# Which tiles share a round of A at the start: tiles 1 and 2 of layer 1 together, and layer 1 three tiles ahead of layer 3 from the first pair on

## The chip, the core and the metric

The kernel runs on one core of one Trainium2 chip, as one launch. The metric is device time in microseconds of a whole execution; the median of three runs before the change is 2122.01 us (2117.99 to 2125.99). TensorE is called PE below, VectorE DVE, ScalarE ACT, GpSimd POOL, and SyncE SP, which issues most DMAs.

## The reference, cut to what matters

The input is a sequence of 2048 rows of 576 values. Four layers are applied one after the other, each with a layer norm before it and a residual sum after it:

```
x = x + A(layernorm(x))     # layer 1
x = x + B(layernorm(x))     # layer 2
x = x + A(layernorm(x))     # layer 3
x = x + B(layernorm(x))     # layer 4
```

A is a local attention with 32 heads of 18: `qkv = x @ wqkv`, then each row attends to itself and to the seven rows that lie 2, 4, ... 14 rows before it, then `@ wo`. B walks the sequence in 64 segments of 32 rows. It has 32 heads of 128. For each segment it puts 8 memory rows ahead of the 32 rows, computes q, k, v, scores with softmax, and the output projection with `Wo`; the first 8 output rows are the memory of the next segment, so segment s+1 cannot begin before segment s has ended. Both A layers use the same weights, and so do both B layers.

## The kernel before

**Steps of B.** The main loop runs over 69 steps. In step t, layer 2 handles segment t (lane 0) and layer 4 handles segment t-5 (lane 1; `DLY=5`), side by side in the same matmuls. A step has the q and k projection of 11 groups of heads (`qk`, lines 908 and 911), the v projection (`vpass`, line 955), scores and softmax for two halves of the heads (`scores`, lines 995 to 1005, and `softmax`, lines 844 to 865), probabilities times v (`pv`, line 1046), and the output projection (`oproj`, line 1070). All weights of B stay in SBUF.

**Rounds of A.** A works on tiles of 64 rows, two steps of B each. One call of `a_tile` is a round, with one or two tiles (`parts`, pairs of layer and tile number). With two tiles, each matmul of the projection (line 570) has 128 columns in place of 64, so both tiles share the weight loads. The weights of A do not stay in SBUF: `wload` brings them as ten strips through `ring`, which has two buffers; strips 0 to 6 are wqkv and 7 to 9 are wo. The first use takes them from a place inside `wo`, where they are put at the start; the second and third use gather them again from the inputs, and the third also stores a packed copy; from the fourth on one DMA fetches the packed copy. In a round the attention (`a_attend`) runs tile after tile: products of q and k in `big` (one buffer), sums over heads on PE (line 678), softmax, a spread of the weights back over the channels on PE (line 703), products with v, and sums. `a_out` then applies wo (line 747), adds the residual, stores x, and makes the normed input of B (`xnb`) through a second layer norm (line 469). A tile needs the last 14 rows of k and v of the tile before it, in `halo1` or `halo3`.

**Which round has which tiles.** `trace` (line 1138) makes the list `its`. Three rounds hold one tile each: 0, 1 and 2 of layer 1. Then tile j+3 of layer 1 is paired with tile j of layer 3 for j = 0, 1, 2. A round with tile 6 alone follows (`EXTRA`), and from there tile j+4 is paired with tile j of layer 3. In the rounds marked late (the second entry of an item), the wo part of the layer 1 tile is held over (`self.pend`) and done together with the layer 3 tile of the next round; so from tile 6 on one `a_out` has two tiles as well. There are 36 rounds and 38 wo parts.

**What sets the order.** Nothing is issued in the order of the source. Every piece is registered with `pl.op`: engine, planned duration, priority, what it depends on, and what buffers it takes. `_Plan.run` (line 93) then plays the whole program through once with these durations, lets each engine take the ready piece of the lowest priority number, and emits instructions in that order. So the order on each engine is fixed when the program is built. The priorities come from the table `PR` (line 1180): some 40 entries, with separate values for the first 12 steps (`_e`) and the last 8 (`_l`), picked by `_at`. PE has three array layouts in this kernel: full (F), four column groups (C: v projection, scores, line 678) and four row groups (R: `pv`, line 703); `mode` in `pl.op` names them, and the planner prefers to stay in one.

Of the kernel before, what the change touches and what calls it, by code (L numbers as in the profile page):

```python
# [27 lines left out]
T = 64  # L28
NS = T // SEG
# [213 lines left out]
AD_ = ("ACT", "DVE")  # L243


def _at(t):
    x = "_e" if t < EARLY else "_l" if t >= NSTEP - LATE else ""
    return {k: PR.get(k + x, v) for k, v in PR.items() if k[-2:] not in ("_e", "_l")}


class _K:
    def __init__(self, ctx, tc, A_x, A_wqkv, A_wo, B_mem0, B_Wq, B_Wk, B_Wv, B_Wo, out):
        self.ctx, self.tc, self.nc = ctx, tc, tc.nc
        self.A_x, self.A_wqkv, self.A_wo = A_x, A_wqkv, A_wo
        self.B_mem0, self.B_Wq, self.B_Wk, self.B_Wv, self.B_Wo = B_mem0, B_Wq, B_Wk, B_Wv, B_Wo
        self.out = out
        _, self.S, d = A_x.shape
        assert d == D and self.S % P == 0
        assert B_Wq.shape[1] == NH and B_Wq.shape[2] == P and B_mem0.shape[1] == NM
        self.NT = self.S // T  # L260
        self.NSEG = self.S // SEG
        self.dly = DLY
        self.nsteps = self.NSEG + self.dly
        assert self.nsteps == NSTEP
        self.scale_b = float(P) ** -0.5
        self.pl = _Plan()
        self.halo = {}


    def pool(self, name, bufs, space=bass.MemoryType.SB):  # L270
        return self.ctx.enter_context(self.tc.tile_pool(name=name, bufs=bufs, space=space))
# [251 lines left out]
    def a_tile(self, parts, late_, dep):  # L523
# [1 line left out]
        nc, pl = self.nc, self.pl  # L525
        m = len(parts)
        n = m * T
        jt = parts[0][1] if m == 1 and parts[0][0] == 1 else 9
        early = jt < 2
        p = _at(NS * parts[-1][1] + (NS if parts[-1][0] == 3 else -LEAD))  # L530
        due, span = (NS * jt - p["a1"], p["a1s"]) if jt < 3 else (NS * parts[-1][1] + (8 if parts[-1][0] == 3 else 0) - p["a"], p["asp"])

        def pr(f):
            return due - span * (1.0 - f)
# [23 lines left out]
        for b in range(14):  # L558
# [15 lines left out]
                      uses=[xn, *w] + ([] if fresh else [ps]), lat=None if c == 3 or b == 13 else 0.0, mm=5)  # L574
            if fresh and 0 < part < 3:
                for l, (layer, j) in enumerate(parts):
                    hin = self.halo.get(layer)

                    def hcopy(e, part=part, l=l, j=j, hin=hin):
                        h = dst[part].t[:, :, l, 0:HALO]  # L580
                        if j == 0:
                            nc.vector.memset(h, 0.0)
                        else:
                            self.copy(e, h, hin[0].t[:, part - 1])
                    got[part, "h", l] = pl.op("DVE" if j == 0 else ("POOL", "ACT") if early else "POOL", 0.25, hcopy, pr(Q[1]),
                                              [o] if j == 0 else [o, hin[1]], uses=[dst[part]] if j == 0 else [dst[part], hin[0]])
# [17 lines left out]
                    got[part, "r"] = pl.op(AD_, _evac(n), evr, pr(Q[1] + 0.08), [o], uses=[ps, dst[part]])  # L604
        pend, self.pend, out = self.pend, None, []
        dep = None
        for l, (layer, j) in reversed(list(enumerate(parts))):
            if j + 1 < self.NT:
                hk = pl.buf(f"halo{layer}")

                def hsave(e, hk=hk, l=l):
                    self.copy(e, hk.t[:, 0], kT.t[:, :, l, T:T + HALO])
                    self.copy(e, hk.t[:, 1], vT.t[:, :, l, T:T + HALO])
                oh = pl.op(("POOL", "ACT") if early else "POOL", 0.5, hsave, pr(Q[2]), [got[1], got[2], got[1, "r"], got[2, "r"]], acq=[hk], uses=[kT, vT])
                self.halo[layer] = (hk, oh)
            late = layer == 1 and late_
            if layer == 3 and pend is not None:
                oT, o_go = pend[4:6]
            else:
                oT = pl.buf("oT")  # L620
                o_go = pl.op("NONE", 0.0, None, pr(Q[0]), [gates[0], dep], acq=[oT])
            o_o, o_l = self.a_attend(layer, j, l, layer // 2, dst, oT, got, o_go, dep, pr, p[f"A{layer}"], early)
            dep = o_o
            it = (layer, j, xTs[l], o_o, oT, o_go, o_l)
            if late:
                self.pend = it
            else:
                out.append(it)
# [239 lines left out]
    def load_x(self, t):  # L868
# [1 line left out]
        nc, pl = self.nc, self.pl  # L870
        hT = pl.buf("hT")
        self.hT[t] = hT
        gate = pl.op("NONE", 0.0, None, t + _at(t)["lx"], [self.qk_op.get(t - 1)], acq=[hT])
        self.x_in[t] = {l: gate for l in range(2)}
        self.gate[t] = gate
        for l in range(2):
            s = self.lane_seg(t, l)
            if s is None:
# [1 line left out]
            xnb, dep = self.xn_ready[l][s // NS]  # L880
            self.x_in[t][l] = pl.op(("POOL", "ACT"), (0.35, 0.36),
                                    lambda e, l=l, s=s, xnb=xnb: self.copy(e, hT.t[:, :, XC[l]:XC[l] + SEG], xnb.t[:, s % NS]),
                                    t + _at(t)["lx"], [dep, gate], uses=[hT, xnb])
            if l == 0 and t % 2 == 0:
                self.x_ahead = pl.op(("POOL", "ACT"), (0.26, 0.29),
                                     lambda e, s=s, xnb=xnb: self.copy(e, hT.t[:, :, W80:HW_], xnb.t[:, s % NS + 1, :, 0:HW_ - W80]),
                                     t + _at(t)["lx"], [dep, gate], uses=[hT, xnb])
            if s == 0:
                m0 = MC + l * NM
                o = pl.op("ACT", 0.26, lambda e, m0=m0: self.copy(e, hT.t[:, :, m0:m0 + NM], self.mem0T[:]),  # L890
# [220 lines left out]

    def b_step(self, t):
        self.qkt, self.qk_ev, self.PT, self.ot, self.o_ev = {}, {}, {}, {}, []
        pr = {k: v[t % 2] for k, v in _at(t).items() if isinstance(v, tuple) and len(v) == 2}
        if t == 0:
            self.vpass(t, 2, 0.0)
        for g in range(11):
# [20 lines left out]
    def trace(self):  # L1138
# [4 lines left out]
        self.hT, self.x_in, self.mem_in, self.qk_op, self.V, self.v_ev, self.e_, self.gate = {}, {}, {}, {}, {}, {}, {}, {}  # L1143
        self.prologue()
        self.pend = None
        its, n1 = [([(1, j)], False) for j in range(3)], 3
        for j in range(NT):
            if j == EXTRA:
                its.append(([(1, n1)], True))
                n1 += 1  # L1150
            its.append((([(1, n1)] if n1 < NT else []) + [(3, j)], j >= EXTRA and n1 < NT))
            n1 += 1
        nl = 0
        for t in range(self.nsteps):
            while nl < len(its) and t >= (NS * its[nl][0][-1][1] + NS if its[nl][0][-1][0] == 3 else NS * its[nl][0][0][1] - LEAD):
                self.a_tile(*its[nl], self.qk_op.get(t - 1))
                nl += 1
            s = self.lane_seg(t - 1, 1) if t >= 1 else None
            if s is not None and s % NS == NS - 1:
                self.finish_out(s // NS, t + _at(t)["fin"])  # L1160
            for lane in range(2):
                s = self.lane_seg(t, lane)
                if s is not None and s % NS == 0:
                    self.residual(lane, s // NS, self.qk_op.get(t - 1), t + _at(t)["res"])
            if t == 0:
                self.load_x(0)
            self.b_step(t)
        self.finish_out(NT - 1, self.nsteps + _at(self.nsteps)["fin"])
        end, busy = pl.run(LOG)
        if VERBOSE:  # L1170
            print("planned", end, busy)
# [5 lines left out]
OTB = 1  # L1177
QKB = 6
RING = 2
PR = dict(qk=(0.307, -2.303), qkd=(0.12, 0.28), v1=(2.247, 4.528), v0=(-0.308, 18.626), s0=(1.899, 2.891), s1=(-11.667, -3.407),  # L1180
          p0=(-0.616, 1.782), p1=(-13.907, 1.038), o=(8.755, -1.999), od=(-3.184, -15.117), mo=(-19.565, -12.77), xo=(-3.022, -4.107),
          v2=(7.079, 5.525), wF=0.772, wC=-8.688, wR=-13.588, fin=2.628, res=-19.303, ring1=5.502, ring3=6.074, lx=16.523, rr=4.185,
          A1=(-16.669, 7.665, 23.282, 5.794, -6.099, 1.521, 0.493, 2.715), A3=(-15.249, 14.933, -15.849, -0.54, -6.577, -8.48, -12.203,
          1.866), a=3.872, asp=0.383, a1=5.649, a1s=-2.211, ai=13.867, st=4.522, qk_e=(2.072, -2.164), qk_l=(0.078, -3.139), qkd_e=(0.044,
          0.417), qkd_l=(0.162, 0.782), v1_e=(2.993, 3.224), v1_l=(2.805, 4.428), v0_e=(3.193, 17.29), v0_l=(-0.844, 18.276), s0_e=(2.324,
          1.847), s0_l=(2.213, -4.283), s1_e=(-10.888, -6.675), s1_l=(-18.328, -7.242), p0_e=(-5.597, 3.192), p0_l=(-8.936, 4.924),
          p1_e=(-21.304, 0.433), p1_l=(-16.629, -0.599), o_e=(15.149, -4.157), o_l=(8.314, -3.071), od_e=(-3.171, -15.728), od_l=(-3.404,
          -11.041), mo_e=(-18.961, -11.562), mo_l=(-14.457, -5.275), xo_e=(-7.103, -0.127), xo_l=(-5.204, -4.583), v2_e=(5.071, 6.422),
          v2_l=(7.565, 7.768), fin_e=1.864, fin_l=4.742, res_e=-16.965, res_l=-18.727, ring1_e=4.197, ring1_l=3.069, ring3_e=1.646,
          ring3_l=2.117, lx_e=10.885, lx_l=10.081, rr_e=6.184, rr_l=8.012, A1_e=(-10.347, 8.693, 24.271, 2.965, -6.696, 3.593, 1.284,  # L1190
          4.89), A1_l=(-6.983, 9.148, 25.195, 2.508, -11.699, 1.391, -0.388, -0.656), A3_e=(-14.483, 9.409, -19.943, -0.138, -3.201,
          -6.45, -15.079, -1.992), A3_l=(-11.391, 14.366, -19.827, 1.172, 1.674, -9.652, -8.623, -1.438), a_e=3.686, a_l=4.704,
          asp_e=0.219, asp_l=0.428, a1_e=3.433, a1_l=0.801, a1s_e=-0.01, a1s_l=-3.617, ai_e=11.156, ai_l=5.274, st_e=5.12, st_l=4.36)
LEAD = 5
EARLY = 12
LATE = 8
NSTEP = 69
EXTRA = 3
COPY = 2
HOLD = False  # L1200
# [58 lines left out]
```

## Time and profile before

| | |
|---|---|
| median of 3 runs | 2122.01 us |
| span of the profiled execution | 2120.6 us |
| PE busy | 2001.4 us (94%), 57787 matmuls |
| DVE, ACT, POOL busy | 1425.8 us (67%), 1169.1 us (55%), 808.5 us (38%) |
| DMA | 168.14 MB, mean 79 GB/s |
| fetches of strips of A, in packed form | 301 of 320 KB and 35 of 160 KB |

The page cuts the span into 40 slices of 53 us. The row of an engine gives its busy share in tenths. PE is a special case: matmuls are pipelined and each has a modelled end, so PE can be shown busy through a short wait. The start of a matmul to the start of the next is the surer measure. Steps are cut here at the first `qk` matmul of a step: the first is at 71.5 us, the sixth (step 6) at 245.3 us, step 12 at 454.7 us.

### The profile page before, as it was taken

How to read it: one execution, taken by the hardware profiler on the slowest of the kernel's cores; microseconds unless marked ns; L12 is line 12 of the kernel's file. 1: busy time of each engine (PE TensorE's matmuls, PEld its weight loads, DVE VectorE, ACT ScalarE, POOL GpSimd, SP SyncE). 2: the span in 40 equal slices, each digit the busy share in tenths (PEclk: the TensorE clock that was granted, in tenths of full speed). 3: DMA queues.
4: the chain of work that ended last, by engine and by line, in shares of the span. 5: the costliest groups of instructions: out<-in, count | busy, mean ns of one | idle time of the engine just before them, and what ended most of it. 6: DMA issues, size and time to landing. Idle time of an engine off the chain costs nothing. (4 is left out here: it accounts for less than half of the span.)

```text
span 2120.6 us, 126521 instructions
## 1 busy us (share of the span) xinstructions
PE 2001.4 (94%) x57787; PEld 1717.2 (81%) x57787; DVE 1425.8 (67%) x3839; ACT 1169.1 (55%) x2869; POOL 808.5 (38%) x1219
## 2 busy tenths in 40 slices
PE   1689989899999999999999999999999999999988
PEld 0468877788888888888888888888888888888876
DVE  2567756666677777776767667776767776766574
ACT  0345545565555555555556556555555555555553
POOL 2124434544434434434344434444344434322321
PEclk9999999999999999999999999999999999999999
DMA  9542223221222222221222212221222222212220
GB/s 322 158 125 77 66 93 96 81 75 54 68 78 78 76 67 68 70 62 59 69 78 77 75 61 74 66 62 60 75 78 76 69 66 70 67 55 73 65 74 13
DMA packets 100392, 168.14 MB, mean 79 GB/s; under 512 B 16904, under 2 KB 55824, under 8 KB 99728
## 3 DMA queue, kind: packets, MB, share of 16 engines
q1 hardware_dynamic: 94320, 140.88, 21.9%
q0 software_dynamic: 4576, 18.88, 2.6%
q8 instruction: 451, 7.39, 1.4%
q14 instruction: 85, 0.70, 0.1%
q10 hardware_dynamic: 960, 0.30, 0.1%
HBM read 144.06 MB, written 15.96 MB: 75 GB/s over the span
## 5 line engine op out<-in xcount | busy, mean ns | idle before, releaser
L908 PE MATMUL r<-hT,wq 128*128 128x80 bf16 (+1 forms) x8832 | 660.7, 198 | 7.6 <-ACT hT L280 6.6
L908 PE MATMUL r<-hT,wk 128*128 128x80 bf16 (+1 forms) x8832 | 663.3, 199 | 0.0
L908 PEld LDWEIGHTS <-wq 128*128 128x128 bf16 x8832 | 509.7, 99 | 22.3 <-issue 15.4
L280 ACT ACTIVATE qk<-r 128x480 bf16<-128x480 f32 (+2 forms) x688 | 364.6, 530 | 295.4 <-PE r L911 284.2
L911 PE MATMUL r<-hT,wqk_r 128*128 128x160 bf16 (+1 forms) x2208 | 508.0, 230 | 0.0
L908 PEld LDWEIGHTS <-wk 128*128 128x128 bf16 x8832 | 448.2, 100 | 0.0
L1070 PEld LDWEIGHTS <-wo 128*128 128x128 bf16 x11040 | 394.3, 100 | 41.6 <-issue 37.0
L1070 PE MATMUL r<-OT,wo 128*128 128x80 bf16 (+1 forms) x11040 | 411.7, 200 | 9.1 <-ACT OT L280 4.7
L287 POOL TENSOR_TENSOR big<-qT,kT 128x512 bf16<-128x512 bf16 x187 | 313.8, 1686 | 126.2 <-DVE oT L287 87.1
L955 PE MATMUL r<-wv,hT 128*32 128x512 bf16 x5376 | 355.0, 383 | 4.6 <-POOL hT L282 4.1
L287 POOL TENSOR_TENSOR ex<-ex,sum 128x320 bf16<-128x320 bf16 x136 | 105.8, 778 | 568.0 <-DVE sum L855 363.6
L955 PEld LDWEIGHTS <-hT 128*32 128x32 bf16 x6720 | 162.5, 96 | 140.2 <-POOL hT L282 4.3
L844 DVE TENSOR_REDUCE nmx<-r 128x8 f32<-128x320 f32 x276 | 133.7, 484 | 169.4 <-PE r L999 168.4
L280 ACT ACTIVATE V<-r 128x512 bf16<-128x512 f32 x281 | 167.6, 598 | 108.3 <-PE r L955 107.9
L911 PEld LDWEIGHTS <-wqk_r 128*128 128x128 bf16 x2208 | 220.1, 100 | 0.0
L280 ACT ACTIVATE OT<-r 128x320 bf16<-128x320 f32 (+1 forms) x401 | 145.6, 425 | 108.0 <-PE r L1046 107.6
L280 ACT ACTIVATE big<-r 128x384 bf16<-128x384 f32 (+1 forms) x316 | 117.9, 438 | 135.1 <-PE r L703 130.8
L287 POOL TENSOR_TENSOR xn<-x,st 128x256 bf16<-128x256 f32 x124 | 75.5, 629 | 271.4 <-DVE st L475 158.7
L570 PE MATMUL r<-xn,ring 128*128 128x128 bf16 (+1 forms) x2450 | 164.7, 215 | 10.6 <-DMA ring<-in_A_wqkv_dram 7.6
L570 PEld LDWEIGHTS <-ring 128*128 128x128 bf16 x2450 | 133.2, 98 | 19.5 <-DMA ring<-in_A_wqkv_dram 8.4
L845 DVE TENSOR_TENSOR r<-r,nmx 128x320 f32<-128x320 f32 x276 | 137.9, 500 | 9.5
L955 PE MATMUL r<-wv_r,hT 128*32 128x512 bf16 x1344 | 133.0, 381 | 0.0
(149 smaller groups left out, 2834.5 us busy)
## 6 DMA issues: line engine op xcount, KB each, us to landing
ring<-strip SPq DMA_DIRECT2D x301, 320.0 KB, 3.1
ring<-strip SPq DMA_DIRECT2D x35, 160.0 KB, 2.2
x1T<-x SPq DMA_DIRECT2D x32, 160.0 KB, 3.2
x<-x1T SPq DMA_DIRECT2D x32, 160.0 KB, 2.5
x3T<-x SPq DMA_DIRECT2D x32, 160.0 KB, 3.2
x<-x3T SPq DMA_DIRECT2D x32, 160.0 KB, 3.0
wo<-in_B_Wo_dram POOLq DMA_DIRECT2D x4, 1152.0 KB, 10.9
wq<-in_B_Wq_dram POOLq DMA_DIRECT2D x2, 2048.0 KB, 19.8
```

The source lines that it names most:

```text
L280: nc.scalar.activation(out=out, in_=in_, func=ACT.Copy, scale=1.0 if scale is None else scale)
L287: (self.nc.vector if e == "DVE" else self.nc.gpsimd).tensor_tensor(out=out, in0=in0, in1=in1, op=op)
L570: nc.tensor.matmul(ps.t[:, c * n:(c + 1) * n], lhsT=view()[:, kc, w0:w0 + P], rhs=xn.t[:, kc, 0:n], start=(kc == 0), stop=(kc == 4))
L844: nc.vector.tensor_reduce(out=m, in_=v, axis=AX.X, op=ALU.max, negate=True)
L845: nc.vector.tensor_tensor(out=v, in0=v, in1=m.unsqueeze(len(shp) - 1).to_broadcast(shp), op=ALU.add)
L908: nc.tensor.matmul(pv[:, hh, wi, a:b], lhsT=self.Wb[wi][0][:, kc, h * P:(h + 1) * P], rhs=hT.t[:, kc, a:b], start=(hh == 0 and wi == 0 and ...
L911: nc.tensor.matmul(pv[:, hh, :, a:b], lhsT=self.Wb[0][1][:, h * P:(h + 1) * P], rhs=hT.t[:, 4:6, a:b], start=False, stop=(hh == n - 1), sk ...
L955: nc.tensor.matmul(ps.t[c * 32:(c + 1) * 32, :], lhsT=l, rhs=w, start=(kc == 0), stop=(kc == 4))
L1070: nc.tensor.matmul(psY.t[:, mb * W80 + c0:mb * W80 + c1], lhsT=self.wo[:, w0:w0 + P], rhs=self.OT[:, h % 16 // 4 * 8 + h // 16 * 4 + h % 4 ...
```

## The change

The list of rounds becomes: tile 0 of layer 1 alone; tiles 1 and 2 of layer 1 in one round (`twin`); tile 3 alone, with its wo part held over; and then tile j+4 of layer 1 with tile j of layer 3 for all j, held over as long as there are layer 1 tiles. There are 35 rounds and 35 wo parts. All layer 1 rounds are registered at step 0, and their priorities come from `a1` and `a1s`. In the twin round the halo of the second tile is copied inside the round, from the last 14 rows of the first, and the two tiles are attended to in rising order. `_at` becomes the method `at` with the same rule. Nearly every number of `PR` is another one; what is computed, the sizes of all buffers, `DLY` and the planner are as before.

```
@@ a_tile
-        jt = parts[0][1] if m == 1 and parts[0][0] == 1 else 9
+        jt = parts[0][1] if parts[-1][0] == 1 else 9
+        twin = m == 2 and parts[1][0] == 1
-        p = _at(NS * parts[-1][1] + (NS if parts[-1][0] == 3 else -LEAD))
-        due, span = (NS * jt - p["a1"], p["a1s"]) if jt < 3 else (...)
+        p = self.at(NS * parts[-1][1] + NS if parts[-1][0] == 3 else 0)
+        due, span = (NS * jt - p["a1"], p["a1s"]) if jt < 9 else (...)
...
             if fresh and 0 < part < 3:
                 for l, (layer, j) in enumerate(parts):
+                    if twin and l == 1:
+                        continue
...
-        for l, (layer, j) in reversed(list(enumerate(parts))):
+        if twin:
+            for part in (1, 2):
+                got[part, "h", 1] = pl.op(("POOL", "ACT"), 0.25, lambda e, part=part: self.copy(
+                    e, dst[part].t[:, :, 1, 0:HALO], dst[part].t[:, :, 0, T:T + HALO]), pr(Q[1]), [got[part], got[part, "r"]], uses=[dst[part]])
+        for l, (layer, j) in list(enumerate(parts))[::1 if twin else -1]:
@@ trace
-        its, n1 = [([(1, j)], False) for j in range(3)], 3
-        for j in range(NT):
-            if j == EXTRA:
-                its.append(([(1, n1)], True))
-                n1 += 1
-            its.append((([(1, n1)] if n1 < NT else []) + [(3, j)], j >= EXTRA and n1 < NT))
-            n1 += 1
+        its = [([(1, 0)], False), ([(1, 1), (1, 2)], False), ([(1, 3)], True)]
+        its += [(([(1, j + 4)] if j + 4 < NT else []) + [(3, j)], j + 4 < NT) for j in range(NT)]
...
-            while nl < len(its) and t >= (NS * its[nl][0][-1][1] + NS if its[nl][0][-1][0] == 3 else NS * its[nl][0][0][1] - LEAD):
+            while nl < len(its) and t >= (NS * its[nl][0][-1][1] + NS if its[nl][0][-1][0] == 3 else 0):
@@ PR: nearly all entries, two lines of them
-          v2=(7.079, 5.525), wF=0.772, wC=-8.688, wR=-13.588, fin=2.628, res=-19.303, ring1=5.502, ring3=6.074, lx=16.523, rr=4.185,
...
+          2.879), p1=(-9.458, 0.493), o=(9.054, -2.393), od=(-2.489, -17.439), mo=(-22.332, -6.705), xo=(2.489, -5.463), v2=(9.677, 6.68),
+          wF=1.098, wC=-6.492, wR=-19.856, fin=2.968, res=-20.105, ring1=7.1, ring3=5.418, lx=7.005, rr=7.518, A1=(-18.916, 7.279, 17.403,
...
```

More of the change, by code (lines that the diff above doesn't have):

```diff
@@ L243 @@
 AD_ = ("ACT", "DVE")
-def _at(t):
-    x = "_e" if t < EARLY else "_l" if t >= NSTEP - LATE else ""
-    return {k: PR.get(k + x, v) for k, v in PR.items() if k[-2:] not in ("_e", "_l")}
 class _K:
@@ L263, in __init__ @@
         self.nsteps = self.NSEG + self.dly
-        assert self.nsteps == NSTEP
         self.scale_b = float(P) ** -0.5
@@ L267, in __init__, with at @@
         self.halo = {}
+    def at(self, t):
+        x = "_e" if t < EARLY else "_l" if t >= self.nsteps - LATE else ""
+        return {k: PR.get(k + x, v) for k, v in PR.items() if k[-2:] not in ("_e", "_l")}
     def pool(self, name, bufs, space=bass.MemoryType.SB):
@@ L527, in a_tile @@
         n = m * T
-        jt = parts[0][1] if m == 1 and parts[0][0] == 1 else 9
+        jt = parts[0][1] if parts[-1][0] == 1 else 9
+        twin = m == 2 and parts[1][0] == 1
         early = jt < 2
-        p = _at(NS * parts[-1][1] + (NS if parts[-1][0] == 3 else -LEAD))
-        due, span = (NS * jt - p["a1"], p["a1s"]) if jt < 3 else (NS * parts[-1][1] + (8 if parts[-1][0] == 3 else 0) - p["a"], p["asp"])
+        p = self.at(NS * parts[-1][1] + NS if parts[-1][0] == 3 else 0)
+        due, span = (NS * jt - p["a1"], p["a1s"]) if jt < 9 else (NS * parts[-1][1] + 8 - p["a"], p["asp"])
         def pr(f):
@@ L872, in load_x @@
         self.hT[t] = hT
-        gate = pl.op("NONE", 0.0, None, t + _at(t)["lx"], [self.qk_op.get(t - 1)], acq=[hT])
+        gate = pl.op("NONE", 0.0, None, t + self.at(t)["lx"], [self.qk_op.get(t - 1)], acq=[hT])
         self.x_in[t] = {l: gate for l in range(2)}
@@ L882, in load_x @@
                                     lambda e, l=l, s=s, xnb=xnb: self.copy(e, hT.t[:, :, XC[l]:XC[l] + SEG], xnb.t[:, s % NS]),
-                                    t + _at(t)["lx"], [dep, gate], uses=[hT, xnb])
+                                    t + self.at(t)["lx"], [dep, gate], uses=[hT, xnb])
             if l == 0 and t % 2 == 0:
@@ L886, in load_x @@
                                      lambda e, s=s, xnb=xnb: self.copy(e, hT.t[:, :, W80:HW_], xnb.t[:, s % NS + 1, :, 0:HW_ - W80]),
-                                     t + _at(t)["lx"], [dep, gate], uses=[hT, xnb])
+                                     t + self.at(t)["lx"], [dep, gate], uses=[hT, xnb])
             if s == 0:
@@ L1113, in b_step @@
         self.qkt, self.qk_ev, self.PT, self.ot, self.o_ev = {}, {}, {}, {}, []
-        pr = {k: v[t % 2] for k, v in _at(t).items() if isinstance(v, tuple) and len(v) == 2}
+        pr = {k: v[t % 2] for k, v in self.at(t).items() if isinstance(v, tuple) and len(v) == 2}
         if t == 0:
@@ L1159, in trace @@
             if s is not None and s % NS == NS - 1:
-                self.finish_out(s // NS, t + _at(t)["fin"])
+                self.finish_out(s // NS, t + self.at(t)["fin"])
             for lane in range(2):
@@ L1163, in trace @@
                 if s is not None and s % NS == 0:
-                    self.residual(lane, s // NS, self.qk_op.get(t - 1), t + _at(t)["res"])
+                    self.residual(lane, s // NS, self.qk_op.get(t - 1), t + self.at(t)["res"])
             if t == 0:
@@ L1167, in trace @@
             self.b_step(t)
-        self.finish_out(NT - 1, self.nsteps + _at(self.nsteps)["fin"])
+        self.finish_out(NT - 1, self.nsteps + self.at(self.nsteps)["fin"])
         end, busy = pl.run(LOG)
@@ L1179 @@
 RING = 2
-PR = dict(qk=(0.307, -2.303), qkd=(0.12, 0.28), v1=(2.247, 4.528), v0=(-0.308, 18.626), s0=(1.899, 2.891), s1=(-11.667, -3.407),
-          p0=(-0.616, 1.782), p1=(-13.907, 1.038), o=(8.755, -1.999), od=(-3.184, -15.117), mo=(-19.565, -12.77), xo=(-3.022, -4.107),
-          v2=(7.079, 5.525), wF=0.772, wC=-8.688, wR=-13.588, fin=2.628, res=-19.303, ring1=5.502, ring3=6.074, lx=16.523, rr=4.185,
[L1183 to L1193, printed above, removed]
@@ new lines @@
+PR = dict(qk=(3.783, 0.155), qkd=(0.199, 0.477), v1=(4.892, 7.836), v0=(3.548, 18.665), s0=(-2.685, 4.017), s1=(-9.056, 1.59), p0=(-0.194,
+          2.879), p1=(-9.458, 0.493), o=(9.054, -2.393), od=(-2.489, -17.439), mo=(-22.332, -6.705), xo=(2.489, -5.463), v2=(9.677, 6.68),
+          wF=1.098, wC=-6.492, wR=-19.856, fin=2.968, res=-20.105, ring1=7.1, ring3=5.418, lx=7.005, rr=7.518, A1=(-18.916, 7.279, 17.403,
+          5.452, -8.146, 6.433, -9.706, 10.409), A3=(-13.279, 16.34, -6.218, 2.183, -7.94, -9.492, -8.605, 1.028), a=3.218, asp=0.562,
+          a1=2.899, a1s=-10.007, ai=27.891, st=10.554, qk_e=(2.743, -1.602), qk_l=(0.759, -11.13), qkd_e=(0.081, 0.665), qkd_l=(0.415,
+          0.024), v1_e=(3.026, 4.014), v1_l=(4.436, 5.046), v0_e=(2.999, 20.034), v0_l=(-3.077, 21.6), s0_e=(1.017, -0.389), s0_l=(-1.583,
+          -3.871), s1_e=(-8.707, -15.639), s1_l=(-18.842, -7.525), p0_e=(-1.746, -0.267), p0_l=(-8.473, 6.83), p1_e=(-23.96, 0.064),
+          p1_l=(-15.946, 9.717), o_e=(18.52, -0.169), o_l=(4.748, -7.24), od_e=(-2.215, -21.06), od_l=(-0.276, -15.013), mo_e=(-21.392,
+          -13.46), mo_l=(-16.326, -7.362), xo_e=(-3.901, -3.782), xo_l=(-6.958, -4.725), v2_e=(7.075, 15.138), v2_l=(10.523, 10.66),
+          fin_e=2.211, fin_l=5.28, res_e=-19.552, res_l=-14.597, ring1_e=3.783, ring1_l=-4.257, ring3_e=0.982, ring3_l=-0.066,
+          lx_e=14.553, lx_l=18.481, rr_e=2.821, rr_l=8.232, A1_e=(-10.356, 12.005, 19.379, 1.568, -7.801, 5.176, -0.499, 5.826),
+          A1_l=(-18.492, 9.463, 27.304, 0.684, -9.422, 3.305, 1.801, -3.168), A3_e=(-15.55, 10.284, -22.423, -1.624, -1.923, -4.881,
+          -21.494, 2.027), A3_l=(-18.572, 10.291, -26.039, -0.447, 3.244, -10.826, -16.043, -1.036), a_e=3.772, a_l=5.234, asp_e=0.216,
+          asp_l=0.647, a1_e=3.024, a1_l=-3.669, a1s_e=0.167, a1s_l=-5.581, ai_e=18.942, ai_l=8.995, st_e=6.988, st_l=5.478)
@@ L1196 @@
 LATE = 8
-NSTEP = 69
 EXTRA = 3
```

## The prediction

> **What bounds the kernel now.** I read the page's slices first, then busy time by stretches cut at the steps, then the waits, then the order of instructions in a steady pair of steps. The slices of the page:
>
> ```profile
> PE   1689989899999999999999999999999999999988
> POOL 2124434544434434434344434444344434322321
> ```
>
> PE is full from the eleventh slice on; only the start is thin. The busy time by stretches, cut at the steps, puts numbers on it. Columns are the stretch, its length, PE's busy time with matmuls, the granted clock, the DMA share and GB/s. Steps 0 to 5:
>
> ```profile
> 71.50:109.40 37.90, 30.51 (x841) 0.86 0.60 173
> 109.40:142.90 33.50, 24.43 (x780) 0.92 0.50 147
> 142.90:166.10 23.20, 23.20 (x758) 0.96 0.30 92
> 166.10:190.70 24.60, 24.12 (x788) 1.00 0.20 61
> 190.70:213.40 22.70, 19.92 (x715) 1.00 0.24 73
> 213.40:245.30 31.90, 31.86 (x892) 1.00 0.34 103
> ```
>
> Steps 6 to 11, and a steady pair of steps:
>
> ```profile
> 245.30:284.00 38.70, 31.16 (x883) 0.92 0.21 66
> 284.00:317.30 33.30, 33.28 (x874) 0.94 0.23 73
> 317.30:348.00 30.70, 28.86 (x858) 1.00 0.26 81
> 348.00:385.00 37.00, 33.87 (x920) 1.00 0.38 118
> 385.00:424.80 39.80, 35.07 (x922) 0.91 0.20 64
> 424.80:454.70 29.90, 29.83 (x856) 1.00 0.22 70
> ...
> 993.90:1053.70 59.80, 59.73 (x1705) 1.00 0.23 70
> ```
>
> A steady pair of steps takes 59.80 us with 0.07 us idle, so PE's own work sets it, and DVE, ACT and POOL with 67, 55 and 38% of the span lie beside it. Steps 6 to 11 take 209.4 us, where three steady pairs would take 179.4: 30 us more. The idle there is 209.4 - 192.1 = 17.3 us; the missing clock, length times what it falls short of 1 (38.7 x 0.08, 33.3 x 0.06, 39.8 x 0.09), is 8.7 us; the rest is extra work of A. The same sums for steps 0 to 5: 7.4 + 9.1 + 0.5 + 2.8 = 19.8 us idle, and 37.9 x 0.14 + 33.5 x 0.08 + 23.2 x 0.04 = 8.9 us of clock.
>
> [...] The order on PE, columns start, length, instruction:
>
> ```profile
> 1014.34 1.05 PE L955 MATMUL r<-wv,hT 128*32 128x512 bf16 x16
> 1015.21 0.39 PE L955 MATMUL r<-wv_r,hT 128*32 128x512 bf16 x4
> 1015.53 0.89 PE L1070 MATMUL r<-OT,wo 128*128 128x80 bf16 x20
> ```
>
> Four groups of the v projection take 0.87 us from start to start, 0.218 each; the fifth is followed by another layout after 0.32. A switch costs 0.10 us. [...]
>
> **The change, part by part.** It settles at build time, so the order of instructions can be counted in both programs.
>
> *The work.* Matmuls go from 57787 to 57642: one wqkv pass (70) and three wo parts (75) fewer. The columns are the same, 64 for each tile; by starts in steady pairs a matmul of 64 columns takes 29 ns and one of 128 takes 56, so a merged pair gains 2 ns, and 145 of them 0.3 us. 16 strip fetches fall away (7 and 3 x 3), with DMA at 22% in the steady part, hidden behind PE: nothing.
>
> *Steps 12 to 56.* Both programs have the same matmuls in these 45 steps, kind by kind, and on PE nearly the same sequence. One place differs. Before, shown here from v projection to spread with the layouts ahead:
>
> ```
> before: C V20 | F LN5 qkvA10 | R pv48 | C V20 | F oproj20 qkvA10 oproj40 | R pv48 | F oproj100 | R spread8
> after:  C V40 | R pv48 | F LN5 qkvA10 oproj80 | R pv48 | F qkvA10 oproj80 | R spread8
> ```
>
> Two switches fewer, 26 in place of 28 for a pair; over the 45 steps 586 in place of 630. 44 x 0.10, and starts between these kinds counted one by one give 0.226 for a pair: 22 pairs, 5.0 us gained. DVE, ACT and POOL have the same instructions there, a few in exchanged places.
>
> *Steps 6 to 11.* Before, these hold the extra round with one tile, the change from separate to joined wo parts, and 30 us of loss. In the changed program the pattern of the steady pairs stands from step 6 on, with 210 wqkv matmuls of 128 columns and 75 of wo for three pairs (before: 70 narrow ones of wqkv more, and 100 narrow with 25 wide of wo), and 93 switches, 9 above three steady pairs of before. 179.4 + 9 x 0.11 = 180.4 us. Its second `pv` comes some 7.2 us after its scores, counted in PE starts, and the softmax between them takes 5.9 to 7.6 us from first score to last transpose in steps 1 to 3 (6.4 in most); so I add 2 us of waits: 182.4, 27.0 us gained.
>
> *Before step 0.* A layer norm of tile 2 now stands ahead of the spread of tile 0, in order on PE. In the trace its transposed input is there at 58.89 us and the spread starts at 59.27; two ACT passes (0.47 and 0.45) and handovers add 1.9 us. On DVE its statistics (3 x 0.23) and four operations on xn (0.54 + 0.55) go ahead of tile 0's products and sums, the chain that ends the 4.8 us wait of the wo part: another 1.9 us. Step 0 starts 3.8 us later.
>
> *Steps 0 to 5.* The counts give 2.7 us more work (tile 3 and the pair of tile 4 are done here, the narrow passes of tiles 1 and 2 merge). Waits that go: 4.1 us for hT of tile 1 in step 1 (its layer norm now has `pv`, 80 `oproj` matmuls and a wo part behind it, 3.6 us), 2.8 us in step 4, and some 3.6 us of the smaller ones in step 1 for strips, `pv` and wo. Waits that come: in step 3 the second `pv` follows its scores by only one piece of wqkv, 1.2 us, against a softmax of 6.4: 5.2 us; in step 4 by 3.1 us: 3.3 us; and step 5 opens 1.7 us behind the layer norm of the first layer 3 tile, whose statistics, normalisation on POOL and copies take 4.2: 2.5 us. Net +0.5. Start of step 6: 3.8 + 2.7 + 0.5 = 7.0 us later. I could not bound it well: if the clock falls behind each of the new waits, 5 us more; if the new waits overlap with DVE's shorter queue, 8 us less.
>
> *The last 12 steps* have the same matmuls and one switch less: nothing.
>
> Sum: +7.0 - 27.0 - 5.0 = -25.0, so a span of 2095.6 from 2120.6. The run that was profiled stood at 2122.37, the median at 2122.01, 1.4 above the span: 2097 us.
>
> **The rivals.** *The start swallows most of it.* More of A sits in steps 0 to 5, where DMA has a share of 0.3 to 0.6 and SP waits in order on landings (tile 1's strips kept PE waiting 5.0 us once). If every strip of the twin round and of tile 3 comes late by what the worst smaller one did (0.6 to 0.9 us, 14 strips) and the clock falls with it, the start loses another 15: 2112. For it: idle and a low clock in just these steps. Against: half as many strips are needed for tiles 1 and 2.
>
> *The start gains too.* If the clock holds in steps 0 to 5 (8.9 us now) and the new waits there are half of my 11.0, the time is 2097 - 14.4 = 2083. For it: the twin round spares PE one set of strip waits. Against: three new waits of 2.5 to 5.2 us are in the order itself.
>
> *A wait in each steady pair, slower than before.* Where V40 now stands, two evacuations of v of 0.6 us stand on ACT ahead of the four of `OT` (0.43 each), and `oproj` comes sooner: 15 matmuls of 56 ns behind `pv` in place of a v projection of 1.1 us. The first `oproj` needs one evacuation, about 1.3 us after `pv` starts, and reaches PE at about 1.35. So 0 to 0.5 us for a pair, 0 to 11 us in all. It decides from 1.2 us a pair (25.0 + 5.0 over 25 pairs); at 1.7 us a pair the time is 2133. Against it: elsewhere in the same pair 9 matmuls stand between `pv` and `oproj`, and by starts the wait there is 0.23 us.
>
> *Nothing comes of it*: the regular pattern of steps 6 to 11 is only planned, and its real waits are those of before, because tiles of layer 3 come no sooner. Then -5.0 + 7.0: 2124. Against it: the steps from 12 on have the same pattern and no waits. That the change doesn't do what it says is ruled out by the counts.
>
> **How the numbers follow.** Forecast 2097 with its own range of 2086 to 2106: 0.60. Start gains too, 2070 to 2086: 0.12. Start swallows, 2106 to 2117: 0.16. Nothing comes of it, 2117 to 2133: 0.07. Slower wait: 0.05. About 0.5%, 10.6 us, is what a measurement of this kernel can tell from no change, so 2111.4 and 2132.6 part the verdicts: faster 0.60 + 0.12 + 0.10 of the third case = 0.82; same 0.06 + 0.07 = 0.13; slower 0.05. A range of 2079 to 2116 leaves out the last two cases, a sliver of the third and the far part of the second, 0.2 in all.
>
> **What would show it.** Right: steps 6 to 11 take 180 to 185 us at a clock near 1.00; a steady pair takes 59.5 to 59.6; step 0 starts near 75 us, step 6 near 252; idle in front of `pv` in steps 3 and 4. Wrong: steady pairs above 60 us with `oproj` waiting for ACT; or step 6 after 265 us; or low clocks still in 250 to 430 us.

## The result, and the profile after

The changed kernel takes 2101.11 us (median of 4 runs, 2099.27 to 2106.00) against 2124.00 us for the kernel before in the same session (median of 4 runs, 2117.99 to 2127.52): a ratio of 0.990, with a 95% interval of 0.987 to 0.993. The span of the profiled execution fell from 2120.6 to 2099.8 us. On the page of the changed kernel, the slices of PE:

```profile
PE   1589899999999999999999999999999999999997
```

A slice is 52.5 us. The first three slices of PE are thin as before, the fifth (210 to 262 us) is at 8 where it was at 9, and from the sixth to the last but one all are full, where the sixth and the eighth were at 8. The busy time by stretches, cut at the steps again, says which steps these are (stretch, its length, PE's busy time with matmuls, granted clock, DMA share, GB/s). Steps 0 to 5 of the changed kernel:

```profile
74.30:110.80 36.50, 29.59 (x819) 0.91 0.57 167
110.80:137.30 26.50, 21.14 (x741) 0.87 0.31 89
137.30:162.80 25.50, 23.45 (x775) 1.00 0.50 144
162.80:197.20 34.40, 29.62 (x854) 0.90 0.28 88
197.20:231.90 34.70, 26.59 (x778) 0.85 0.24 69
231.90:261.20 29.30, 28.94 (x842) 1.00 0.18 57
```

Steps 6 and 11, and the same steady pair of steps as before:

```profile
261.20:292.30 31.10, 31.10 (x874) 1.00 0.29 90
...
412.70:441.40 28.70, 28.70 (x837) 1.00 0.16 47
...
978.30:1037.90 59.60, 59.53 (x1706) 1.00 0.24 70
```

Two opposite things happened. Steps 6 to 11 now look like steady steps: about 31.1 and 28.7 us in turn (step 7 took 29.4), 180.2 us together in place of 209.4, with 0.2 us idle and the full clock. Steps 0 to 5 became longer: steps 3 and 4 took 24.6 + 22.7 = 47.3 us before and take 69.1 now, at a clock of 0.90 and 0.85, and 9.6 of the 21.8 us more are idle time of PE. Summed over the run:

| stretch | before, us | after, us | difference | forecast |
|---|---|---|---|---|
| start of step 0 | 71.5 | 74.3 | +2.8 | +3.8 |
| steps 0 to 5 | 173.8 | 186.9 | +13.1 | +3.2 |
| steps 6 to 11 | 209.4 | 180.2 | -29.2 | -27.0 |
| steps 12 to 56 | 1348.3 | 1341.3 | -7.0 | -5.0 |
| last 12 steps and tail | 317.6 | 317.1 | -0.5 | 0 |
| span | 2120.6 | 2099.8 | -20.8 | -25.0 |

The waits of PE in steps 6 to 11 show what the gain there is. Each line says who waited on which line, for whom, how long in total, how often, and the longest; the kernel before, 245 to 425 us:

```profile
PE r L908 <- ACT hT L280: 3.0, 2, 1.6
...
PE r L1046 <- DVE pt L865: 2.8, 2, 1.7
PE r L747 <- DMA ring<-strip: 2.5, 2, 1.4
PE r L747 <- POOL oT L287: 2.3, 1, 2.3
```

The whole answer for the changed kernel from 262 to 441 us is one line:

```profile
PE r L960 <- issue: 0.2, 1, 0.2
```

No single wait had to be removed. Before, these steps hold a round with one tile and the change to joined wo parts; PE waits there in short pieces on ACT, DVE, POOL and strips alike. In the changed kernel nearly the order of a steady pair stands from step 6 on, and in that order each of these producers has been done in time.

The waits of PE that remain in the changed kernel between 60 and 262 us:

```profile
PE r L1051 <- DVE pt L870: 7.8, 4, 2.9
...
PE r L569 <- DMA ring<-strip: 3.6, 3, 1.9
...
PE r L752 <- DMA ring<-in_A_wo_dram: 2.1, 2, 1.5
PE r L683 <- POOL big L285: 2.1, 1, 2.1
```

The first line is `pv` waiting for the last transpose of the softmax. 5.1 us of it lie in steps 3 and 4, as forecast; 2.3 lie in step 1 and were not forecast, and neither were the other three lines.

### The profile page after: what moved, and what is told of

Read it like the earlier page. It is cut to its first block, busy times and chain, and to the rows that moved or that the text cites. A ratio compares the mean times of both kernels' runs of the same rounds, so it can differ in the third digit from the quotient of the medians.

```text
span 2099.8 us, 126220 instructions
## 1 busy us (share of the span) xinstructions
PE 1989.5 (95%) x57642; PEld 1716.4 (82%) x57642; DVE 1398.9 (67%) x3819; ACT 1189.9 (57%) x2890; POOL 788.0 (38%) x1212
## 3 DMA queue, kind: packets, MB, share of 16 engines
q1 hardware_dynamic: 92016, 136.13, 21.8%
## 4 chain that ended last, share of the span: by engine, by line
PE 91%; DMA 4%; DVE 3%; ACT 1%; issue 1%; SPq 0%; POOL 0%; ACTq 0%; DVEq 0%; POOLq 0%
PE r L913 29%; PE r L1075 18%; PE r L960 18%; PE r L916 7%; PE r L569 6%; PE r L1051 3%; PE r L752 2%; PE r L467 2%; PE r L708 1%; PE r L1010 1%; DMA x<-in_B_mem_dram 1%; PE r L683 1%; PE r L1004 1%; PE r L1000 1%; DMA wo<-in_A_wqkv_dram 1%; ACT OT L278 1%
## 5 line engine op out<-in xcount | busy, mean ns | idle before, releaser
L278 ACT ACTIVATE qk<-r 128x480 bf16<-128x480 f32 (+3 forms) x714 | 378.9, 531 | 269.9 <-PE r L916 260.6
L1075 PE MATMUL r<-OT,wo 128*128 128x80 bf16 (+1 forms) x11040 | 407.5, 200 | 7.7 <-ACT OT L278 4.5
L285 POOL TENSOR_TENSOR big<-qT,kT 128x1024 bf16<-128x1024 bf16 x185 | 310.5, 1685 | 185.8 <-DVE oT L285 155.1
L278 ACT ACTIVATE big<-r 128x384 bf16<-128x384 f32 (+1 forms) x294 | 112.3, 442 | 128.3 <-PE r L708 126.2
```

Of the source, the lines that this page charges most:

```text
L278: nc.scalar.activation(out=out, in_=in_, func=ACT.Copy, scale=1.0 if scale is None else scale)
L285: (self.nc.vector if e == "DVE" else self.nc.gpsimd).tensor_tensor(out=out, in0=in0, in1=in1, op=op)
L1075: nc.tensor.matmul(psY.t[:, mb * W80 + c0:mb * W80 + c1], lhsT=self.wo[:, w0:w0 + P], rhs=self.OT[:, h % 16 // 4 * 8 + h // 16 * 4 + h % 4 ...
```

## The experiments

The first four runs part the change in its two halves, the rounds (all of the change but the table) and the table `PR`, and then the rounds and the table in two again. The other eight take up the loss in steps 0 to 5. Every kernel computes the whole of the reference. Ratios are to the kernel before in the same session (2124.38, 2127.37 and 2130.72 us in the three sessions).

### The old rounds with the new table

```
  open/before.py with the new priorities:
- PR = dict(qk=(0.307, -2.303), ...
+ PR = dict(<all entries of the changed kernel>)
```

> The kernel before with the priority table of the kernel after and its own list of rounds. In the built order, steps 12 to 56 have 586 changes of array layout (the kernel after has 586, the kernel before 630), and steps 6 to 11 still hold the extra round. Theory (two gains that add: the list of rounds empties steps 6 to 11, the table takes 0.2 us off each steady pair): steady pairs 59.6 us, steps 6 to 11 still 205 to 212 us, span about 2115 us. Rival (the table alone makes the start regular, the list does nothing): steps 6 to 11 at 180 to 188 us, span about 2095 us.

Measured: 2134.49 us, 1.0055 [1.0033, 1.0077]. The stretches: steps 0 to 5, and a steady pair:

```profile
72.10:260.60 188.50, 156.46 (x4761) 0.91 0.36 106
...
1011.50:1071.10 59.60, 59.53 (x1709) 1.00 0.23 70
```

The pair has the new 59.60, as the theory had it, and steps 6 to 11 are no better than before (214.3 us, 2.3 above the theory's range). The start was missed by both sides, 188.5 us in place of 173.8, and with it the span, 2133.0 us. The early entries of the new table do not suit the old rounds, and the kernel is slower than before.

### The new rounds with the old table

```
  changed kernel:
- PR = dict(qk=(3.783, 0.155), ...
+ PR = dict(<all entries of the kernel before>)
```

> The kernel after with the priority table of the kernel before. 630 changes of layout in steps 12 to 56. Theory: steady pairs 59.8 us, steps 6 to 11 at 179 to 184 us, span about 5 us above the kernel after, 2105 us, if the order of steps 0 to 5 under this table costs what it costs in the kernel after. Rival (the gain is the table's): steps 6 to 11 above 195 us, span 2115 us or more.

Measured: 2119.20 us, 0.9981 [0.9972, 0.9990]. The first two stretches are steps 0 to 5 and 6 to 11:

```profile
74.30:272.70 198.40, 163.48 (x4790) 0.90 0.33 97
272.70:452.50 179.80, 179.60 (x5108) 1.00 0.23 69
```

Steps 6 to 11 are empty of waits with the old table too, so that gain belongs to the rounds. Steps 12 to 56 stay at 1347.8 us, so that gain belongs to the table. And the start costs 198.4 us, so the span of 2105 us that the theory expected was missed by 15.6: in steps 0 to 5 the new table is worth 11.5 us with the new rounds, where it costs 14.7 with the old ones.

### The old rounds with the new table's steady entries alone

```
  open/before.py: the entries without a suffix from the changed kernel,
  the entries _e (first 12 steps) and _l (last 8) as they were
```

> The kernel before with only those entries of the table exchanged that hold for the middle steps (no first twelve, no last eight). 589 changes of layout in steps 12 to 56, start nearly as before. Theory (a change of layout costs 0.10 to 0.11 us): steady pairs 59.56 to 59.60 us, span 2115 to 2116 us. Rival (the evacuations queue on ACT in front of the output projection and take it back): steady pairs 59.8 us or more, span 2120 us or more.

Measured: 2120.39 us, 0.9976 [0.9964, 0.9987]. A steady pair, and steps 12 to 56:

```profile
999.10:1058.70 59.60, 59.53 (x1709) 1.00 0.25 70
460.90:1803.20 1342.30, 1340.06 (x38267) 1.00 0.24 70
```

6.0 us less in steps 12 to 56 (1348.3 before), by these entries alone. Steps 6 to 11 took 214.9 us, 5.5 more than before, although their own entries did not change: the planner places the pieces of neighbouring steps together, and its order on PE in steps 5 and 6 is another one. Whether that order costs the 5.5 us is not shown; the execution that was profiled (2124.34 us) lay 4 us above the median of its kernel. So the profiled span (2122.6) is not lower and misses the forecast of 2115 to 2116; the medians are lower, by 0.24%.

The place in the pair is the one that the forecast named. The order on PE in the changed kernel (start, length, instruction):

```profile
997.24 1.04 PE L960 MATMUL r<-wv,hT 128*32 128x512 bf16 x16
998.10 0.39 PE L960 MATMUL r<-wv_r,hT 128*32 128x512 bf16 x4
998.42 0.54 PE L1051 MATMUL r<-pt,V 32*128 32x48 bf16 x48
```

The second v projection of the step stands directly ahead of `pv`, not ahead of `oproj`, and the pair has two layout switches fewer: a regular pair went from 59.78 to 59.60 us, 0.18 us less.

### The new rounds without the shared one

```
- its = [([(1, 0)], False), ([(1, 1), (1, 2)], False), ([(1, 3)], True)]
+ its = [([(1, j)], False) for j in range(3)] + [([(1, 3)], True)]
```

> The kernel after with tiles 1 and 2 in a round each, and tile 3 alone and pairs three tiles later as in the kernel after: one pass over wqkv more in the start. Theory (what empties steps 6 to 11 is that layer 1 is a tile further ahead and the wo parts are joined from the first pair on, the sharing only pays for it): steps 6 to 11 at 180 us, the start later than in the kernel after by the extra pass, 2 us of PE work and up to 8 us of waits for seven more gathered strips, span 2102 to 2110 us. Rival (the sharing carries the gain): span 2115 us or more.

Measured: 2120.78 us, 0.9986 [0.9972, 0.9999]. Steps 0 to 5, steps 6 to 11, and step 4:

```profile
68.40:276.40 208.00, 169.91 (x4863) 0.85 0.35 103
276.40:457.10 180.70, 180.06 (x5111) 1.00 0.24 69
194.80:245.70 50.90, 35.15 (x877) 0.76 0.28 81
```

Being three tiles ahead with joined wo parts from the start is enough to clean steps 6 to 11, as the theory said. But the total fell to the rival: with tiles 1 and 2 apart, one more round must fit into steps 0 to 5, and step 4 alone takes 50.9 us. What PE waited for there:

```profile
PE r L683 <- POOL big L285: 7.6, 3, 5.4
PE r L1051 <- DVE pt L870: 3.0, 1, 3.0
```

Step 0 starts 5.9 us earlier (68.4), steps 0 to 5 are 21.1 us longer: the shared round is worth 15 us net at the start, with this table. A table made for the unshared rounds was not tried.

### The softmax of steps 3 and 4, planned longer

The table of waits names `pv` on the transposes first. In these two experiments the planner is told that the last transpose of a softmax in steps 3 and 4 reaches PE 4 us, or 2 us, later, so that it puts other work ahead of `pv`. No instruction changes, only the order.

```
-   prio, [o, after], acq=..., uses=...)
+   prio, [o, after], acq=..., uses=..., lat=4.0 if t in (3, 4) else None)
```

> The kernel after with one edit: the planner is told, in steps 3 and 4 alone, that the last transpose of a softmax reaches PE 4 us later, so it puts other work between the scores and the matmuls of probabilities times v. The order up to step 3 is that of the kernel after. Theory (in steps 3 and 4 the order itself exposes the softmax, and each exposure costs its wait and the clock that falls after it): waits on the transposes in steps 3 and 4 fall from 7 us to 2 us or less, the two steps take 60 to 64 us in place of 69.1, span 2091 to 2095 us. Rival (the two steps are bound by the chain of tile 3, tile 4 and the first layer 3 tile on POOL, DVE and the strips; PE then waits in another place): the two steps take 67 us or more, and the span stays within 3 us of 2099.8 us.

> The same edit with 2 us in place of 4. Theory: between the kernel after and the 4 us variant, 62 to 67 us for steps 3 and 4. Rival: 67 us or more.

Measured with 4 us: 2099.98 us, 0.9872 [0.9853, 0.9891]; with 2 us: 2103.55 us, 0.9886 [0.9862, 0.9910]. Neither interval parts from the changed kernel's. The waits between 60 and 262 us with 4 us:

```profile
PE r L1051 <- DVE pt L870: 2.8, 2, 2.5
...
PE r L752 <- DMA ring<-strip: 3.1, 1, 3.1
```

The waits on transposes fell from 7.8 to 2.8 us, and in steps 3 and 4 alone from 5.1 (not the 7 that the expectation names) to nothing. But a wait of 3.1 for a strip of wo, which wasn't in the list before, came up, and steps 3 and 4 went from 69.1 to 66.2 us only, PE's idle time there from 12.9 to 11.4. The 66.2 lies between the theory (60 to 64) and the rival (67 or more), nearer to the rival, and the span of 2098.7 us is the rival's: once one wait is filled, the next producer is late. With 2 us there was no wait on transposes in these steps either; they took 70.1 us, on the rival's side, with 4.5 us of waits for strips of wqkv.

Not all of such a difference comes from the order. In steps 0 to 2 PE, DVE, ACT and POOL run the same order in these two kernels and in the changed one, and these steps took 90.0, 88.5 and 88.5 us: two traces can differ by 1.6 us for no reason of the plan.

### POOL's pieces in two more rounds, open to DVE and ACT

In the rounds of tiles 0 to 2, the products of q and k, the halo copies and the products of the layer norm may go to DVE or ACT where they would else go to POOL. This edit allows the same in the round of tile 3 and in the first pair (called the wider choice below).

```
- early = jt < 2
+ early = jt < 4 or parts[-1] == (3, 0)
```

> The kernel after with DVE and ACT allowed to take POOL's pieces (products of q and k, halo copies, layer norm products) in the rounds of tile 3 and of the first pair too, not only in the first two rounds. Theory of the softmax: the wait of the second matmul block of probabilities times v in step 3 stays (2.9 us), so the two steps gain 2 to 4 us at most, from the 2.1 us wait for products on POOL. Rival (the chain of the first layer 3 tile on POOL bounds steps 3 and 4): the two steps take 62 us or less, span 2093 us or less.

Measured: 2101.60 us, 0.9874 [0.9851, 0.9897]. The wait for POOL's products is gone, the waits on transposes in steps 3 and 4 fell from 5.1 to 3.4 us, and 3.5 us of waits for strips of wo came in their place. Steps 3 and 4 took 66.9 us, 2.2 less and so within the theory; step 0 began 1.2 later (75.5), in the same order. In the whole time there is no difference from the changed kernel that these runs can tell.

### Tile 2's layer norm behind tile 0

```
- gate = pl.op("NONE", ..., [o_x, gate], ...)
+ gate = pl.op("NONE", ..., [o_x, gate, self.x1_stored[0] if twin and l == 1 else None], ...)
```

> The kernel after with the layer norm of tile 2 made to wait for the store of tile 0, so it no longer stands ahead of tile 0's spread on PE; the planner then orders steps 1 to 5 anew. Theory: step 0 starts 2.8 to 3.8 us sooner, at 70.5 to 71.5 us in place of 74.3; what steps 1 to 5 take is open, since their order differs. Rival (the start of step 0 is set by the weights' DMAs, not by this chain): step 0 starts at 73.5 us or later.

Measured: 2105.13 us, 0.9895 [0.9875, 0.9916]. Step 0 began at 72.3, 2.0 us earlier, between the theory (70.5 to 71.5) and the rival (73.5 or later). One start says little, though. With the combinations below, four kernels have this edit and the same order on PE, DVE, ACT and POOL up to step 0; they began it at 71.2, 72.3, 72.4 and 75.8 us. The changed kernel and the four without this edit share one order up to there as well, and began step 0 at 74.3 (twice), 74.9, 75.5 and 78.7. The middles lie 2.5 us apart, and each group alone spreads over 4 us or more. Nothing of the gain is left at the end: step 4 now takes 43.3 us, with one wait of 8.9 on a transpose.

### Combinations

Four kernels join these edits: the layer norm behind with 4 us; the layer norm behind with the wider choice and 2 us, and the same with 4 us; and the wider choice with 4 us.

```
norm_behind_late_pv_4:  gate as in norm_behind,                  lat=4.0
norm_early_late_pv_2:   gate as in norm_behind, early as above,  lat=2.0
norm_early_late_pv_4:   gate as in norm_behind, early as above,  lat=4.0
early_late_pv_4:                                early as above,  lat=4.0
```

> The layer norm of tile 2 behind the store of tile 0, and the 4 us of the softmax edit in steps 3 and 4, on the kernel after. With the first edit alone step 0 started at 72.3 us, steps 1 to 3 took 80.5 us (kernel after 86.3), and step 4 took 43.3 us with one wait of 8.9 us on a transpose. Theory (that wait is the planner's softmax being too short, and can be filled): step 4 takes 32 to 35 us, span 2090 to 2094 us. Rival (the chain of tiles in step 4 comes late whatever stands ahead): step 4 takes 38 us or more, span 2098 us or more.

> The same with DVE and ACT allowed to take POOL's pieces in the rounds of tile 3 and the first pair, and 2 us in place of 4. Theory: steps 3 and 4 together 58 to 62 us (kernel after 69.2), span 2087 to 2093 us. Rival: other waits take their place, 65 us or more, span 2097 us or more.

> All three edits, with 4 us. Theory: steps 3 and 4 together 58 to 62 us, span 2087 to 2093 us, unless the later start of the first layer 3 tile moves the loss into steps 5 to 7, which would take over 92 us (kernel after 89.7).

> The kernel after with DVE and ACT for the rounds of tile 3 and the first pair, and the 4 us of the softmax edit, without the edit of the layer norm. Each alone took 2.5 to 3 us off steps 3 and 4. Theory: the two remove different waits and add: 62 to 64 us for the two steps, span 2093 to 2096 us. Rival (both only shift the same chain): 66 us or more.

| kernel | median, us | ratio | start of step 0 | steps 3 + 4 | steps 6 to 11 |
|---|---|---|---|---|---|
| changed kernel | 2101.11 | 0.9899 [0.9869, 0.9928] | 74.3 | 69.1 | 180.2 |
| layer norm behind, 4 us | 2102.80 | 0.9871 [0.9856, 0.9886] | 75.8 | 67.9 | 180.3 |
| layer norm behind, wider choice, 2 us | 2098.02 | 0.9857 [0.9837, 0.9878] | 72.4 | 67.4 | 180.0 |
| layer norm behind, wider choice, 4 us | 2137.10 | 1.0031 [1.0017, 1.0045] | 71.2 | 67.4 | 212.0 |
| wider choice, 4 us | 2116.37 | 0.9933 [0.9916, 0.9949] | 78.7 | 73.6 | 185.0 |

The kernel with the layer norm behind, the wider choice and 2 us has the lowest median of all kernels here; its interval overlaps with that of the changed kernel, so it isn't shown to be better (the first row was measured in a session of its own, each ratio against the kernel before in the same session). The edits do not add. No kernel of the four reached the span that its theory gave, and where 58 to 64 us were expected for steps 3 and 4, 67.4 to 73.6 came. With the layer norm behind and 4 us, step 4 fell from 43.3 to 33.6 us as expected, but step 3 grew from 26.4 to 34.2. The wider choice with 4 us is slower than either alone. The case with all three at 4 us is the most telling. Its steps 6 to 11, and their first two waits:

```profile
260.40:472.40 212.00, 193.00 (x5163) 0.94 0.22 65
...
PE r L1051 <- DVE pt L870: 11.6, 5, 3.4
PE r L752 <- DMA ring<-strip: 5.1, 3, 2.0
```

It enters step 6 at 260.4 us, 0.8 earlier than the changed kernel, and has the same rounds and table. But the planner's order for steps 6 to 11 is not the one of the steady pairs, and the loss of the kernel before is back: 212.0 us with 19 us idle. So the new rounds make the regular order possible; they do not by themselves bring it about.

## Why the prediction was right, and where it was off

The time came out at 2101, within the likeliest case's own range of 2086 to 2106 us and 4 us above the forecast of 2097. That it came so near is in part luck: steps 0 to 5 were 9.9 us dearer than forecast, and smaller misses of 1.0, 2.2, 2.0 and 0.5 us in the other stretches went the other way. Step by step:

*Steps 6 to 11: right in mechanism and size.* 182.4 forecast, 180.2 measured; the 2 us that were added for waits behind the scores did not come. That the rounds do this, and not the table, is shown by the two crossed runs (179.8 with the old table, 214.3 with the old rounds), and that being ahead does it, and not the sharing, by the run without sharing (180.7). The last combination bounds the claim: it holds where the planner finds the regular order.

*Steps 12 to 56: right.* Starts counted one by one gave 0.226 us for a pair and 5.0 in all; a regular pair went from 59.78 to 59.60, 22 of them 4.0 us. Most of the rest was not forecast: several pairs of the kernel before are longer than a regular one, by 3.3 us together, and those of the changed kernel by 0.8. The rival of a wait in each steady pair is refuted: `oproj` has no wait there, the pair has 0.07 us idle.

*Before step 0: 2.8 where 3.8 was forecast.* With tile 2's layer norm behind, the middle start came 2.5 us earlier. Since starts in one and the same order spread over 4 us, these runs cannot tell 2.8 from 3.8.

*Steps 0 to 5: this is the term that was mis-sized.* The prediction had work +2.7 and waits +0.5; the measured change is +13.1. PE's idle time went from 19.8 to 27.6 us, +7.8. The clock, which the forecast kept as it was, is counted from the stretches that the record shows at half clock, and from PE's busy time in them. In steps 0 to 5 of the kernel before these are:

```profile
79.75:86.58 6.83, 4.87 (x128) 0.50 0.53 131
93.40:96.81 3.41, 3.41 (x40) 0.50 0.30 46
137.78:144.61 6.83, 4.00 (x68) 0.50 0.32 115
```

And in those of the changed kernel:

```profile
82.11:88.94 6.83, 4.45 (x93) 0.50 0.46 114
126.48:133.31 6.83, 3.92 (x114) 0.50 0.53 161
187.92:194.75 6.83, 5.20 (x104) 0.50 0.13 44
211.81:222.05 10.24, 7.47 (x153) 0.50 0.31 87
```

PE worked 12.3 us at the granted clock of 0.50 before and 21.0 now. Half of that, an estimate from the 0.50, is lost, 6.1 and 10.5 us: 4.4 more. (Length times shortfall, as the prediction reckons it, gives 8.9 and 15.4 us; it also counts the halved clock of idle time, which stands in the idle time already.) Work, what remains, went up by about 1. The prediction had named a lower clock as something it could not bound well, "5 us more", and left it out of the sum; 4.4 came.

The larger part of the miss is the idle time. The waits that were forecast to come were over-estimated: `pv` in step 3 waited 2.9 us (5.2 forecast), in step 4 2.2 (3.3), and the 2.5 at the opening of step 5 did not come. But those that were to go away did not all go: step 1 gave only 3.7 us (9.1 idle before, 5.4 now; 7.7 forecast), because `pv` waits 2.3 us there for a transpose and the wo part 2.1 for its strips, where these were 1.0 and 0.8 before. And producers that were not on the list kept PE waiting in steps 3 and 4: 2.1 us for POOL's products, 3.6 for strips. The runs that filled the wait on the transposes, or gave POOL's pieces to other engines, show it again: steps 3 and 4 stayed at 66 to 74 us each time.

The clock can be seen directly. Stretches of 3 us in step 3 of the changed kernel:

```profile
184.00:187.00 3.00, 1.30 (x17) 1.00 0.66 209
187.00:190.00 3.00, 0.45 (x33) 0.65 0.41 125
190.00:193.00 3.00, 3.00 (x35) 0.50 0.00 0
193.00:196.00 3.00, 3.00 (x104) 0.71 0.02 5
```

PE worked 1.75 of the 6 us before 190, in small pieces between waits of 0.6, 0.9 and 2.9 us. Then it has work, and runs it at half speed: the clock is 0.50 from 187.9 to 194.7 us. The sixteen matmuls of `wv` take 1.90 us there against 1.04 in the steady pair above. The wait of 2.9 us ended at 189.5; half of the 5.2 us from there to 194.7, 2.6 us, is an estimate, from the granted 0.50, of what the halved clock cost on top of the waits. So these waits cannot be added up by their own length alone.

*The rival "the start swallows most of it" was half right.* It put 15 us on top, 2112; the start took 8.9 more than forecast (step 6 at 261.2, between the 252 named as a sign of being right and the 265 named as a sign of being wrong). The lower clock that it named came. Its mechanism, every strip late, was a part only: 3.6 us for strips of wqkv, 2.1 for wo.

Some readings in the prediction's working do not hold, though the forecast does not hang on them. The row of slices is full from the ninth slice on, not the eleventh. Counted by PE's busy time at half clock, the missing clock in steps 6 to 11 was 5.8 us and not 8.7. In step 1 the list of waits has 2.6 us for strips, `pv` and wo, not 3.6. And 25 pairs at 1.7 us would add 42 us to 2097, so 2139 and not 2133.

Not settled: why each of the two tables costs the other's rounds 11 to 15 us in steps 0 to 5. The runs show the size, and that the edits that were tried do not add; a table made for one of the mixed kernels would tell whether this is more than a matter of fitting.

## What to carry to other kernels

When a planner decides the order, look for the stretch that is not yet in the steady pattern, and count what it costs above the steady one: here 30 us in six steps, nearly all of which could be had by starting the steady pattern earlier. The price is paid where the work is moved to; size it with the clock that is granted there: here waits of 0.6, 0.9 and 2.9 us close together cost their own length, and the granted clock was 0.50 for 6.8 us, which cost an estimated 2.6 us on top. And test the schedule's parts crosswise: rounds alone gave 0.2%, the table alone lost 0.6%, both together gained 1.0%.

## What the runs showed of the hardware

In steps 3 and 4 of the changed kernel no wait was longer than 2.9 us, and the granted clock was 0.50 twice, for 6.8 us (187.9 to 194.7) and for 10.2 (211.8 to 222.1). The 3.4 us ahead of each of the two, and two stretches of the same length that were nearly as thin and were followed by a clock of 1.00:

```profile
184.50:187.92 3.42, 1.26 (x17) 1.00 0.58 181
208.40:211.81 3.41, 1.57 (x77) 1.00 0.02 5
...
225.46:228.88 3.42, 1.71 (x38) 1.00 0.63 183
228.88:232.29 3.41, 1.69 (x30) 1.00 0.66 191
```

PE is shown busy for 1.26 and 1.57 us in the two stretches ahead of a halved clock, and for 1.71 and 1.69 us in the two others. In steps 6, 7 and 10 of the kernel before, where the granted clock was 0.92, 0.94 and 0.91, the longest wait was 2.3 us. So in these steps the clock was halved where the waits were short. What decides it is not shown. The ends of matmuls are modelled, so these busy times are those of the profile.

The same steady pair (steps 30 and 31) took 59.60 us in each of four kernels with the new steady entries: the changed kernel, the old rounds with the new table, the old rounds with its steady entries alone, and the new rounds without the shared one. In the kernel before it took 59.80. So two layout switches more or less, some 0.2 us in 60, are seen in one profile, where the intervals of the whole runs' ratios above reach 0.1 to 0.3% to either side.
